# Sliding-window attention followed by a dense eight-expert MLP on one core: batch 1's token blocks offered in units of 256, and batch 2's casts and turns issued two half-blocks later

## The chip, the cores and the metric

One core of one Trainium2 chip runs the whole program in one launch. The metric is the device time of one execution in microseconds. Three runs of the kernel before took 1062.36, 1057.84 and 1061.02 us, so the median is 1061.02 us. The execution that the profiler recorded took 1060.31 us; its span, from the first to the last instruction, is 1058.5 us.

## The reference

The inputs q, k and v have 8 batches, 8 heads, 576 positions and 64 channels. Attention is causal with a window of 128 positions and a linear bias by head. Its output, 4608 tokens of 512 channels, is the input x of eight experts, all of which see every token; their outputs are weighted by a routing matrix P that eight row and column normalisations produce.

```python
scores = scale * np.matmul(q, k.transpose(0, 1, 3, 2))
mask = (rel >= 0) & (rel < window)
scores = np.where(mask, scores + bias[None], -1000000000.0)
attn = np.exp(scores)
...
logits = x @ w_gate
...
for e in range(E):
    h = np.maximum(x @ w1[e], 0.0)
    ye = h @ w2[e]
    out += P[:, e:e + 1] * ye
```

## The kernel before

**Stages.** Attention runs batch by batch, and experts 0 and 1 are computed between its pieces, so that TensorE (PE) has matmuls to do while ScalarE (ACT) and VectorE (DVE) work on the softmax. Their results go to memory (`ysp`). Then come the gating, the eight normalisations and, for most of the span, experts 2 to 7. The change touches the attention stage alone, and of it batches 1 and 2.

**Half-blocks.** A batch has five blocks of keys (`kb` 0 to 4; four of 128, one of 64) and two groups of four heads (`u`). One pair (kb, u) is a half-block; the loop of L627 goes through 80 of them, ten to a batch, numbered `at = 2 * kb + u`. This text writes (1,5) for half-block 5 of batch 1. In each, the next half-block's work is started and this one's is finished, in a fixed order that is written out by hand: when the next half-block has u = 0, the scores of both its head groups (PE, L363); the exponential of the next (ACT, L386); a first piece of filler (about 1 us); the mask multiplication of the next (DVE, L398); the values matmuls of this one (PE, L409) with the division by the sum (DVE, L436 and L437); if u is 0, the transposition of the previous block's output into `xT` (L447; for batches 0 to 2 and 7 by PE and a DVE copy, for the others by a DMA); the rest of the filler; and then, at the loop's end, loads, casts and turns for later batches. Every engine and every DMA queue works through its own instructions in this order; an instruction that waits holds up what stands behind it on its engine.

**Casts and turns.** q and k of a batch are loaded as float32 (`load_qk`, SP's queue, 1 MB each). `cast_qk(b, j)` turns a quarter of them to float16, k on ACT and q on DVE (L247, L245). For batches 0 to 2, `turn_pe` transposes a quarter on PE into a PSUM tile, which ACT (k, L326) or DVE (q, L324) copies to its place; for the later batches `turn_qk` does it by two DMA transposes on SP's queue, and POOL and DVE bring the result into order (`order_qk`). The last 64 positions of q and k travel in a tile of their own; for batches 0 to 2 PE turns it when the next half-block is (b,5), that is in (b,4), and ACT copies it out (L320). `load_qk(2)` is issued in (0,3), `load_qk(3)` in (1,3) and `load_qk(4)` in (2,3).

**Filler.** `Filler` holds units (expert, first block, number of 128-token blocks). A unit has eight L1 atoms (one eighth of the hidden width each: four matmuls over its tokens, then a ReLU on ACT, L109) and one L2 atom for each block (eight matmuls, then a copy on DVE, L499 or L495). `take` gives the next atom: two L1, then an L2 if there is one; a unit is begun, the first of the list that is ready, when no L1 atom is left and at most two L2 atoms are. A unit is ready when all its blocks are (`ready`, L659 to L664: in batches 0 to 2, block 4b + n counts as ready from the end of (b,2n), and all four from the end of (b,8)) and its expert is allowed (expert 1 from the end of (1,4)). `backlog` is the planned time of all that is ready (0.87 us for an L1 atom of four blocks, in proportion for fewer, and 1.74 us for an L2 atom), and `budget` spreads it evenly over the half-blocks up to (b,8) in batches 0 to 2, or up to the next batch's first.

**PSUM.** Filler, values, turns and gates share four PSUM buffers (`pmm`), so a matmul group can also wait for the evacuation of an earlier one. The scores have two buffers of their own (`psS`).

Of the kernel before, what the change touches and what calls it, by code (L numbers as in the profile page):

```python
# [14 lines left out]
def kernel(  # L15
# [25 lines left out]
    NG = Ntok // GT  # L41
# [161 lines left out]
    if True:  # L203
# [33 lines left out]
        def cast_qk(b, j):  # L237

            if j == 0:
                c16s[b] = per.tile([P, 2, RI, H, Dh], FP16, name=f"c16_{b}", tag="a8", bufs=8)  # L240
            for n in (1, 0):
                src = raw[b][n][:, 2 * j : 2 * j + 2, :].rearrange("p h (i d) -> p i h d", i=RI)
                to = c16s[b][:, n, :, 2 * j : 2 * j + 2, :]
                if n == 0:
                    nc.vector.tensor_copy(out=to, in_=src)  # L245
                else:
                    nc.scalar.copy(out=to, in_=src)  # L247
            if j == NDT - 1:
                raw.pop(b)
# [52 lines left out]
        def turn_pe(b, kq, j):  # L302

            wide = j == NDT
            ps = aps.tile([P, RI, P], FP32 if wide else FP16, name=f"psT_{b}_{kq}_{j}", tag="pmm", bufs=4)
            for i in range(RI):
                if wide:
                    src = tails[b][:, 2 * i : 2 * i + 2, :]
                else:
                    src = c16s[b][:, kq, i, 2 * j : 2 * j + 2, :]  # L310
                nc.tensor.matmul(
                    out=ps[:, i, :],
                    lhsT=src.rearrange("p h d -> p (h d)"),
                    rhs=ident32 if wide else ident,
                    is_transpose=True,
                    start=(i == 0),
                    stop=(i == RI - 1),
                )
            if wide:
                nc.scalar.copy(out=QKT[b][2], in_=ps)  # L320
                return
            to = QKT[b][kq][:, j].rearrange("p (r i) -> p r i", i=RI)
            if kq == 0:
                nc.vector.tensor_copy(out=to, in_=ps.rearrange("p i r -> p r i"))  # L324
            else:
                nc.scalar.copy(out=to, in_=ps.rearrange("p i r -> p r i"))  # L326
# [36 lines left out]
        def scores(b, kb, u):  # L363

            nk, nn = sizes(kb)
            ps = aps.tile([P, 2, 2, 2 * P], FP32, name=f"psS_{b}_{kb}_{u}", tag="psS", bufs=2)
            both = kb < NKB - 2
            for y in range(2):
                j = 2 * u + y
                for hb in range(2):  # L370
                    n = 2 * P if both else nk
                    nc.tensor.matmul(  # L372
                        out=ps[0:nk, hb, y, 0:n],
                        lhsT=cols(b, 1, j, hb, kb),
                        rhs=cols(b, 0, j, hb, kb, 1 + both),
                    )
                for hb in range(2):
                    if nn and not both:
                        nc.tensor.matmul(
                            out=ps[0:nk, hb, y, nk : nk + nn],  # L380
                            lhsT=cols(b, 1, j, hb, kb),
                            rhs=cols(b, 0, j, hb, kb + 1),
                        )
            pss[b, kb, u] = ps

        def exps(b, kb, u):  # L386
            nk, nn = sizes(kb)
            ps = pss.pop((b, kb, u))
            pt = asb.tile([P, 4, 2 * P], FP16, name=f"pt_{b}_{kb}_{u}", tag="pt", bufs=4)
            nc.scalar.activation(  # L390
                out=pt[0:nk, :, 0 : nk + nn],
                in_=ps[0:nk, :, :, 0 : nk + nn].rearrange("p a y n -> p (a y) n"),
                func=AF.Exp,
                scale=scale,
            )
            pts[b, kb, u] = pt

        def masks(b, kb, u):  # L398
            nk, nn = sizes(kb)
            pt = pts[b, kb, u]  # L400
            hs = slice(4 * u, 4 * u + 4)
            w = nk + nn
            nc.vector.tensor_tensor(  # L403
                out=pt[0:nk, :, 0:w], in0=pt[0:nk, :, 0:w], in1=mask[0:nk, hs, 0:w], op=ALU.mult
            )
# [38 lines left out]
        def by_pe(b):  # L444
            return b < XPE or b == B - 1
# [53 lines left out]
            nc.vector.tensor_copy(out=yo, in_=ps)  # L499
            stores.append((e, blk, yo))  # L500

        spans = [(0, 2), (2, 2)] + [(4 * g, 4) for g in range(1, NG)]
        order = [(0, 0), (0, 1)]
        for n in range(2, len(spans)):
            order += [(0, n), (1, n - 2)]
# [82 lines left out]
        def some(n):  # L588
            for _ in range(min(n, len(todo))):
                todo.pop(0)()  # L590
# [36 lines left out]
        for n, (b, kb, u) in enumerate(steps):  # L627
            nxt = steps[n + 1] if n + 1 < len(steps) else None
            at = 2 * kb + u
            left = ((8 if b < XPE else 10) - at) % 10 + 1  # L630
            budget = filler.backlog() / (11 if (b, at) == (XPE, 0) else left)
            if nxt:
                if nxt[0] < XPE and nxt[1:] == (RI - 2, 1):
                    turn_pe(nxt[0], 0, NDT)
                if nxt == (1, 0, 0):
                    cast_qk(1, 0)
                    cast_qk(1, 1)
                    for j in range(NDT):
                        turn_pe(1, 1, j)
                        turn_pe(1, 0, j)  # L640
                        if j < 2:
                            cast_qk(1, j + 2)
                        filler.fill(1.0)
                if n == 0:
                    scores(*nxt)
                elif nxt[2] == 0:
                    scores(*nxt)
                    scores(*nxt[:2], 1)
                exps(*nxt)
            got = filler.fill(1.0)  # L650
            if nxt:
                masks(*nxt)
            values(b, kb, u)
            if n > 0 and u == 0 and by_pe(steps[n - 1][0]):
                turn_x(*steps[n - 1][:2])
            if u == 1 and n // 2 + NKB < B * NKB:
                cast_v(n // 2 + NKB)
            filler.fill(budget - got)
            if at == 0 and b > XPE:  # L659
                filler.ready = 4 * b  # L660
            if at < 8 and b < XPE:
                filler.ready = 4 * b + at // 2
            if at == 8 and b < XPE:
                filler.ready = 4 * b + 4  # L664
            if u == 1 and not by_pe(b):
                turn_x(b, kb)
            if u == 1:
                if kb == 1 and b > 0:
                    gates(4 * b - 4, 4 * b)
                if n // 2 + NKB + 1 < B * NKB:  # L670
                    load_v(n // 2 + NKB + 1)
            if b == 0 and at == 1:
                load_weights(1)
            if b == 1 and at == 4:
                filler.allowed.add(1)
                nc.sync.dma_start(out=ysp[0, 0:RI].rearrange("m p d -> p m d"), in_=first_y[0])
            if (b, at) == (0, 3):
                load_qk(2)
            if (b, at) == (0, 7):
                homes(1)  # L680
            if (b, at) == (1, 3):
                homes(2)
            if b == 1 and 3 <= at <= 6:
                cast_qk(2, at - 3)
            if b == 1 and 4 <= at <= 7:
                turn_pe(2, 1, at - 4)
                turn_pe(2, 0, at - 4)
            if 1 <= b < B - 2 and at == 3:
                load_qk(b + 2)
            if 1 <= b < B - 2 and at >= 8:  # L690
                cast_qk(b + 2, at - 8)
            if 2 <= b < B - 1:
                if at < 2:
                    cast_qk(b + 1, at + 2)
                if at == 1:
                    turn_qk(b + 1)
                    order_qk(b + 1, 1, range(NDT))
                if at == 5:
                    turn_tail(b + 1)
                if at in (6, 7):  # L700
                    order_qk(b + 1, 0, range(2 * at - 12, 2 * at - 10))
            if b < B - 1 and at == (1 if b > 1 else 5) and b:
                load_tail(b + 1)
            if 10 * b + at >= 66:
                i = 10 * b + at - 66
                if i % 8 == 0:
                    home_last(2 + i // 8)
                (load_w2 if i % 8 < 4 else load_w1)(2 + i // 8, i % 4, 4)
            if (b, at) == (7, 0):
                todo += sums_of(2, *extras(2))  # L710
            if b == 7 and at >= 5:
                some(1)
# [270 lines left out]
        for n in range(N):  # L983
            g = units[n - 1][0]
# [62 lines left out]
```

## Time and profile before

| what | number |
|---|---|
| median of three runs | 1061.02 us |
| profiled execution | 1060.31 us |
| its span | 1058.5 us |
| DVE busy | 631.7 us (60%) |
| ACT busy | 434.5 us (41%) |
| PE waiting in the span's first 52.9 us, longest: L311 for ACT's cast (L247) | 7.0 us, 3 times |
| PE waiting from 52.9 to 112.85 us, longest: L457 for ACT's copy of the tail (L320) | 2.9 us, once |
| DMA engines' mean busy share, 50 to 60 us | 1.10 |
| the same, 80 to 90 us | 0.00 |

A row of a timeline names the start and the time of an instruction or of several alike, the engine, the source line, the operation, output and inputs, and in square brackets how long the engine had been idle before it and what ended that. PE's rows are modelled at their ends, so times between starts are used for what a group of matmuls costs. Half-blocks are found in PE's timeline by their order: scores of a new block appear in the odd half-blocks, the L473 group (gates) is in the third of batch 1 (it computes batch 0's), and so on. In the profiled execution (1,4) ends near 57.1 us, (1,9) begins with the scores of 76.74 us and (2,9) with those of 112.85 us.

### The profile page before, as it was taken

The numbers are of one execution on the slowest core, as the hardware profiler recorded it, in microseconds if no ns is written. First come the engines' busy times: TensorE is split into PE (matmuls) and PEld (weight loads), VectorE is DVE, ScalarE is ACT, GpSimd is POOL, SyncE is SP. The second block draws the span as 40 slices with busy tenths as digits, with TensorE's granted clock in tenths as the row PEclk, the third lists the DMA queues.
The fourth block names the chain that finished last, engine by engine and source line by source line (L and its number), as shares of the span: only waits on it lengthen the run. The fifth ranks groups of instructions, "written<-read, shape, count | busy, mean of one in ns | idle before, by whom it ended". The sixth has DMA issues, their size and how long they took to land.

```text
span 1058.5 us, 21148 instructions
## 1 busy us (share of the span) xinstructions
PE 1031.1 (97%) x9006; PEld 802.9 (76%) x9006; DVE 631.7 (60%) x1171; ACT 434.5 (41%) x729; POOL 77.4 (7%) x139
## 2 busy tenths in 40 slices
PE   6789999999999999999999999999999999999998
PEld 4455444444544888888888888888888888888887
DVE  4655665655687665655655655655655655555555
ACT  6556555555233333333333333333333333333332
POOL 2112032325100000000000000000000000000000
PEclk9999999999999999999999999999999999999999
DMA  9985599879992501211211210211220220220240
GB/s 226 252 221 139 114 201 218 196 154 177 182 207 70 115 23 49 71 26 46 71 39 33 70 49 23 71 39 32 71 65 7 71 68 3 71 71 1 71 90 20
DMA packets 166110, 98.55 MB, mean 93 GB/s; under 512 B 84960, under 2 KB 157440, under 8 KB 166016
## 3 DMA queue, kind: packets, MB, share of 16 engines
q1 hardware_dynamic: 151280, 79.21, 29.4%
q0 software_dynamic: 14304, 17.84, 10.2%
q8 instruction: 70, 1.15, 0.4%
q14 instruction: 24, 0.20, 0.1%
q10 hardware_dynamic: 432, 0.16, 0.1%
HBM read 87.74 MB, written 19.02 MB: 101 GB/s over the span
## 4 chain that ended last, share of the span: by engine, by line
PE 92%; DMA 4%; SPq 2%; DVE 1%; ACT 1%; issue 0%; POOL 0%; ACTq 0%
PE psh L834 36%; PE psS_m L889 31%; PE psh L102 11%; PE psy L115 10%; DMA v<-in_v_dram 2%; DMA k<-in_k_dram 2%; PE psN L426 1%; PE psS L372 1%; DMA xT<-xsb 1%; SPq L334 1%; SPq L223 0%; SPq L288 0%; PE psy L954 0%; PE psG L473 0%; ACT hT L109 0%
## 5 line engine op out<-in xcount | busy, mean ns | idle before, releaser
L841 ACT ACTIVATE hs<-psh 128x512 f16<-128x512 f32 x432 | 258.0, 597 | 453.2 <-PE psh L834 373.7
L834 PE MATMUL psh<-aux,w1l 128*128 128x256 f16 x2880 | 372.6, 273 | 0.2 <-ACT hs L841 0.2
L834 PEld LDWEIGHTS <-w1l 128*128 128x128 f16 x2880 | 281.7, 98 | 33.3 <-issue 0.5
L889 PEld LDWEIGHTS <-hs 128*128 128x128 f16 x2568 | 251.3, 98 | 29.1
L846 DVE TENSOR_TENSOR hs<-hs 128x1024 f16<-128x1024 f16 x107 | 74.1, 693 | 274.5 <-ACT hs L841 274.3
L889 PE MATMUL psS_m<-w2l,hs 128*128 128x256 f16 x1440 | 186.6, 273 | 0.0
L102 PE MATMUL psh<-xT,w1t 128*128 128x512 f16 (+1 forms) x640 | 141.1, 359 | 4.4 <-DMA xT<-xsb 1.7
L115 PE MATMUL psy<-w2t,hT 128*128 128x512 f16 x576 | 133.8, 379 | 3.4 <-DMA w2t<-in_moe_w_dram 2.8
L818 DVE TENSOR_TENSOR aux<-xT,pbc 128x1024 f16<-128x1024 f16 x108 | 131.4, 1217 | 2.5 <-DMA pbc<-ptd 2.5
L109 ACT ACTIVATE hT<-psh 128x512 f16<-128x512 f32 (+1 forms) x160 | 87.6, 556 | 100.6 <-PE psh L102 99.3
L115 PEld LDWEIGHTS <-hT 128*128 128x128 f16 x576 | 53.7, 98 | 64.6 <-issue 4.8
L102 PEld LDWEIGHTS <-w1t 128*128 128x128 f16 x640 | 57.9, 99 | 53.6 <-issue 6.4
L390 ACT ACTIVATE pt<-psS 128x1024 f16<-128x1024 f32 (+2 forms) x80 | 67.5, 852 | 45.9 <-PE psS L372 37.0
L935 DVE TENSOR_TENSOR acc<-acc,psS_m 128x256 f32<-128x256 f32 (+1 forms) x162 | 74.3, 504 | 12.4 <-PE psS_m L889 11.1
L499 DVE CAST yo<-psy 128x512 f16<-128x512 f32 x68 | 46.9, 690 | 55.5 <-PE psy L115 54.3
L403 DVE TENSOR_TENSOR pt<-pt,mask 128x1024 f16<-128x1024 f16 (+2 forms) x80 | 50.2, 627 | 41.5 <-ACT pt L390 41.4
L889 PE MATMUL psS_m<-more,hs 128*128 128x256 f16 x576 | 74.6, 273 | 0.0
L834 PE MATMUL psh<-aux,w1t 128*128 128x256 f16 x576 | 74.6, 273 | 0.0
L849 DVE TENSOR_TENSOR hs<-hs 128x1024 f16<-128x1024 f16 x107 | 73.2, 684 | 0.0
L834 PEld LDWEIGHTS <-w1t 128*128 128x128 f16 x576 | 56.4, 98 | 6.5
L535 POOL DMA_DIRECT2D w2t<-in_moe_w_dram x2 | 1.8, 878 | 705.2 <-PE psS_m L889 669.8
L426 PEld LDWEIGHTS <-pt 128*128 128x128 f16 (+2 forms) x576 | 28.6, 101 | 26.1 <-DVE pt L403 6.8
(83 smaller groups left out, 657.2 us busy)
## 6 DMA issues: line engine op xcount, KB each, us to landing
pbc<-ptd SPq DMA_DIRECT2D x108, 128.0 KB, 4.5
y<-ysp SPq DMA_DIRECT2D x36, 256.0 KB, 4.7
ysp<-yo SPq DMA_DIRECT2D x68, 128.0 KB, 3.1
v<-in_v_dram SPq DMA_DIRECT2D x32, 256.0 KB, 3.9
out_dram<-acc SPq DMA_DIRECT2D x31, 256.0 KB, 2.4
q<-in_q_dram SPq DMA_DIRECT2D x7, 1024.0 KB, 6.4
k<-in_k_dram SPq DMA_DIRECT2D x7, 1024.0 KB, 9.8
w2t<-in_moe_w_dram POOLq DMA_DIRECT2D x4, 1024.0 KB, 14.7
```

What stands on the lines that cost most here:

```text
L102: nc.tensor.matmul(out=ps[:, 0:nt], lhsT=w1ts[e][:, dt, P * ft : P * ft + P], rhs=xT[:, b0 : b0 + nb, dt, :], start=(dt == 0), stop=(dt == ...
L109: nc.scalar.activation(out=st["hT"][:, ft, 0:nt], in_=ps[:, 0:nt], func=AF.Relu)
L115: nc.tensor.matmul(out=ps, lhsT=st["hT"][:, ft, P * ms : P * ms + P], rhs=w2ts[e][:, ft, :], start=(ft == 0), stop=(ft == NFT - 1),)
L390: nc.scalar.activation(out=pt[0:nk, :, 0 : nk + nn], in_=ps[0:nk, :, :, 0 : nk + nn].rearrange("p a y n -> p (a y) n"), func=AF.Exp, scale ...
L403: nc.vector.tensor_tensor(out=pt[0:nk, :, 0:w], in0=pt[0:nk, :, 0:w], in1=mask[0:nk, hs, 0:w], op=ALU.mult)
L818: nc.vector.tensor_tensor(out=xs(n).rearrange("p (d b t) -> p d b t", d=NDT, b=2), in0=xT[:, 2 * g : 2 * g + 2].rearrange("p b d t -> p d ...
L834: nc.tensor.matmul(out=ps[:, f, :], lhsT=W1L[e][:, dt, P * ft : P * ft + P], rhs=xs(n)[:, HB * dt : HB * dt + HB], start=(dt == 0), stop=( ...
L841: nc.scalar.activation(out=h[n][:, 2 * i : 2 * i + 2, :], in_=ps, func=AF.Relu)
L846: nc.vector.tensor_tensor(out=t[:, NFT : NFT + NF2, :], in0=a[:, 0:NF2, :], in1=a[:, NF2:NFT, :], op=ALU.add)
L849: nc.vector.tensor_tensor(out=t[:, NFT + NF2 : 2 * NFT, :].rearrange("p f n -> p (f n)").rearrange("p (f t) -> p f t", t=P), in0=a[:, :, P ...
L889: nc.tensor.matmul(out=Ms[g, bank][:, half, :], lhsT=left(n, m, f), rhs=W2L[e][RIGHT[m]][:, f, :], start=(e == 2 and f == 0 and half == 0) ...
L935: nc.vector.tensor_tensor(out=a, in0=a, in1=p2, op=op)
```

## The change

Two edits. The first splits the units of blocks 4 to 7, which are batch 1's, into two of 256 tokens for each of the two experts. The order list keeps its rule (expert 1 two units behind expert 0).

```diff
-        spans = [(0, 2), (2, 2)] + [(4 * g, 4) for g in range(1, NG)]
+        spans = [(2 * g, 2) for g in range(4)] + [(4 * g, 4) for g in range(2, NG)]
```

The second moves batch 2's four casts and four turns. Before, cast j is issued at the end of (1,3+j) and turn j at the end of (1,4+j). After, casts 0 and 1 are issued at the end of (1,5); turns 0 and 1 and then cast 2 at the end of (1,6); turn 2 and cast 3 at the end of (1,7); turn 3 at the end of (1,8). The number of casts and turns is the same.

```diff
-            if b == 1 and 3 <= at <= 6:
-                cast_qk(2, at - 3)
-            if b == 1 and 4 <= at <= 7:
-                turn_pe(2, 1, at - 4)
-                turn_pe(2, 0, at - 4)
+            if b == 1 and 5 <= at <= 8:
+                for j in ((), (0, 1), (2,), (3,))[at - 5]:
+                    turn_pe(2, 1, j)
+                    turn_pe(2, 0, j)
+                for j in ((0, 1), (2,), (3,), ())[at - 5]:
+                    cast_qk(2, j)
```

## The prediction

> **What bounds the kernel now.** I read the page first, then PE's waits, then the timeline of the stretch that the edits touch, then that stretch as a window.
>
> ```profile
> PE 1031.1 (97%) x9006; PEld 802.9 (76%) x9006; DVE 631.7 (60%) x1171; ACT 434.5 (41%) x729; POOL 77.4 (7%) x139
> ...
> PE   6789999999999999999999999999999999999998
> ```
>
> PE is busy for 1031.1 of 1058.5 us. Its 27.4 us of idle time lie mostly in the first two slices (26.5 us each), where nothing is changed. An edit that moves PE's work without adding any can win only the idle time of its own stretch.
>
> ```profile
> 52.90:112.85 59.95, 56.05 (x484) 32.45 (x484) 33.87 (x81) 33.44 (x62) 12.77 (x27) 0.97 0.75 185
> 112.85:140.90 28.05, 26.45 (x222) 12.94 (x221) 17.05 (x40) 17.44 (x27) 6.76 (x9) 1.00 0.54 120
> 46.86:52.90 6.04, 3.97 (x73) 2.77 (x73) 5.62 (x15) 2.96 (x3) 0.00 (x0) 1.00 1.15 220
> ```
>
> Windows; the columns are length, busy time of PE, weight load, DVE, ACT and POOL, PE's clock, DMA share and rate. Up to 52.90 us (in half-block (1,4)) both kernels issue the same work; from (2,9), whose scores start at 112.85 us, the planner issues the same again. Between the two lie 3.9 us of idle PE, and the granted clock is 0.97.
>
> ```profile
> 52.49 0.39 PE L426 MATMUL psN<-v,pt 128*128 128x65 f16 x7 [0.38 <-DVE pt L403]
> ...
> 54.62 0.62 ACT L247 CAST c<-k 128x512 f16<-128x512 f32 x1 [2.90 <-DMA k<-in_k_dram]
> 55.14 0.58 ACT L320 CAST tT<-psT 128x512 f16<-128x512 f32 x1
> 55.62 1.03 ACT L390 ACTIVATE pt<-psS 128x1024 f16<-128x1024 f32 x1
> 55.77 0.59 PE L457 MATMUL psX<-ident,xsb 128*128 128x128 f16 x4 [2.89 <-ACT tT L320]
> ```
>
> This is the stall: ACT reached cast 0 of batch 2 at the end of (1,3), k's load landed only at 54.6 us, and the tail's copy and the next exponential stood behind it. PE needed the copy.
>
> **What is saved.** I measure from 52.90 us to 113.95 us, where (2,9)'s filler starts: 61.05 us. Moved to the end of (1,5), the cast no longer stands ahead of the copy. By then k has landed, as (1,5) holds 7 us of filler. Saved: 52.90 to 55.77, 2.87 us. The granted clock is 0.50 from 55.7 to 59.1 us; the groups from 55.77 to 59.35 took 3.58 us, and the same ones later, at full clock, take 0.22 (L457) + 0.45 (two turns) + 0.45 (scores) + 0.87 (two L1 atoms) = 1.99, so 1.59 us are saved if the clock stays up. PE's other waits of the stretch are 0.60 at 64.83, 0.43 at 83.25 and 0.49 at 113.95. Together 5.98 us, the most that can be won.
>
> The Trainium skill (TensorE: Matmul & The Clock Gate, Part 1) has the clock halved after an idle window of about 3.4 us in a free-running count. Here a gap of 2.87 us sufficed, as 52.3 to 55.7 was idle but for 0.4 us. By the page, the 1.59 us would not be in every execution of the kernel before, and the saving between 4.39 and 5.98 us.
>
> **The units.** At the end of (1,4) eight blocks are now ready (expert 0: 4, 5; expert 1: 0 to 5) where there were four (expert 1: 0 to 3). A block costs the planner 0.87 x 8/4 + 1.74 = 3.48 us, so the backlog is 27.84 us instead of 13.92, spread over four half-blocks: (1,5) to (1,8) get 6.96 us each, not 3.48. The ten from (1,9) to (2,8) then share 13.92 us, not 27.84; following `take`: 1.30, 1.30, 1.30, 2.17, 2.61, 0.87, 0.87, 1.74, 1.74 and 0. PE's matmuls hardly cost more: six L1 atoms of 256 tokens take 2.62 us (59.59 to 62.21), three of 512 take 2.59, so 32 x 0.437 - 16 x 0.863 = **+0.2 us**. ACT gets 32 ReLUs of 0.42 (four in 1.69) for 16 of 0.59 (two in 1.18): +4.0 us, beside PE, since ACT is busy for 33.4 of 59.95; without that cover up to +4.0.
>
> **New waits.**
> (a) Expert 0's unit of blocks 4 and 5 comes first, so (1,5) starts with matmuls on block 5, whose transposition is issued just before. Tail copy on ACT 52.1, exponential 52.6, mask 53.66 (1.06 after the exponential, as 55.62 to 56.68 before), division 54.3 and 54.5, DVE's copy to `xT` 54.8 to 55.25. PE has the turn and the scores of block 3 until 53.9. Wait 1.3, with 0.15 ahead of the turn: **+1.45 us**, none if PE arrives later, no more than the old 2.87.
> (b) Turn 3 of batch 2 now stands right ahead of (1,9)'s scores, which need its copies. DVE has a `yo` copy (0.6) and then the q copy (0.6) after the last L2; PE waits **0.7 us** (0 to 1.2, both copies). Before, (1,8) lay between.
> (c) The thin half-blocks. Without filler, four half-blocks took 6.04 us (46.86 to 52.90) with PE idle for 2.07, DVE busy for 93%: 0.52 idle each. With 2.4 us of filler, the eight from 112.85 to 140.90 had 1.60: 0.20 each. Ten of them with 1.39: between 2.0 and 5.2 us. Following the queues by hand I find 1.2 in (2,0), where the ReLUs stand behind a cast and an exponential on ACT, 0.9 in (2,2) to (2,5), and about 2 in (2,8), which has no filler while DVE still has (2,6) and (2,7)'s two `yo` copies and four reorderings (0.55 each). I take **4.0**, nearer the upper row since (2,4) to (2,8) are nearest to it.
> (d) Batch 4's load. SP works in order:
>
> ```profile
> 89.59 5.05 SPq L261 DMA_TRANSPOSE qk<-c  x2
> ...
> 98.39 0.63 SPq L232 DMA_DIRECT2D q<-in_q_dram  x1
> 99.07 1.13 SPq L232 DMA_DIRECT2D k<-in_k_dram  x1
> ```
>
> The transposes wait for batch 3's last cast, in (2,1); k's load stands 9.5 us behind them and lands 9.4 us later, near 108.5. ACT's cast of it, the last thing in (2,8), ran at 108.94: 19.4 us after the casts, with no wait. The fuller (1,5) to (1,8) put (2,1)'s end at about 96.5, and the thin (2,2) to (2,8) last some 15.5 us, not 19.4. So the cast at about 112 waits until 115.4, with (2,9)'s exponential and ReLUs behind it. PE has (2,9)'s filler (2.6 us) and values meanwhile. I take **+1.0** of the 3.5 (bounds 0 and 3.5).
>
> Nothing else of a moved step costs: casts (0.51 ACT, 0.33 DVE) and turns (0.45 PE a pair, 0.5 and 0.6 to copy) are as many as before, they issue no DMA, and `load_qk(3)`, now ahead of the cast's tile, finds free buffers. POOL's 4.6 us of reordering moves 7 us later and ends near 108, ahead of the scores at 112.
>
> **The sum.** 0.2 + 1.45 + 0.7 + 4.0 + 1.0 = 7.35 given back, against 5.98: **+1.4 us**. From (2,9) on PE has the same work and nearly no idle time, so the difference lasts to the end. 1060.31 + 1.4 = 1061.7; the median of the runs lies 0.7 above the profiled execution: **1062.4 us**, a change too small to measure (about 0.5%, 5.3 us, is what a measurement of this kernel can tell from none).
>
> **The rivals.**
> *The thin half-blocks stay full and the load is in time.* (c) at 2.0 and (d) at 0: 4.35 - 5.98 = -1.6, so 1059.4. For it: DVE's average load there, about 85%, leaves room. Against: a half-block with no filler at all.
> *The stall is won and hardly anything given back*: 0.2 + 1.45 - 5.98 = -4.3, 1056.7. It needs (b) to (d) at nothing; three queues speak against it.
> *Slower: ACT's wait for k moves from batch 2's cast to batch 4's.* Place: the end of (2,8). It decides once less than 18.9 us (9.5 + 9.4) lie between (2,1)'s casts and that cast. Price: 3.5 us with nothing to cover it, (c) at 5.2, and a clock window at half speed, 1.59, as the same wait cost before: 0.2 + 1.45 + 0.7 + 5.2 + 3.5 + 1.59 - 5.98 = +6.7, 1067.7. For it: SP's order, and that `load_qk(4)` has no slack now. Against: PE has 2.6 us of filler at that place, where it had none before.
> *It doesn't do what it says*: the casts still meet an unlanded load at (1,5). Then nothing is saved but (b) to (d) are paid: about +5.9 less part of the waits that were counted twice. 54.6 us against 62 speaks against it.
>
> **The numbers.** Forecast 0.48 (1059.5 to 1065), the full half-blocks 0.22, the stall won for nothing 0.08, batch 4's load 0.20, not done 0.02. Faster than 1055.7 takes the second rival and a quieter execution: 0.07. Slower than 1066.3 is the third, the fourth and little of the forecast: 0.21. The rest, 0.72, is no change. Range: from just under the second rival's time to just over the third's, 1056.5 to 1068.
>
> **What would show it.** In the profile after: ACT's L320 right behind the tail's turn with PE idle under 0.3 us there, and clock 1.00 at 56 us (saving); PE's first L102 after the scores near 53.5 waiting for DVE's L465 (a); scores of (1,9) waiting for L324 (b); PE's idle time between about 87 and 113 us (c); ACT's L247 waiting for k near 112 us (d). I am wrong if (1,9) starts far from 87 us, or if PE's idle time from 52.9 us to (2,9) differs from 6 to 7 us by more than 3.

## The result, and the profile after

The changed kernel took 1064.8 us in the median of 16 runs (1061.88 to 1067.18); the kernel before, over 16 runs, 1060.37 us (1056.66 to 1063.49). The ratio is 1.0043, with a 95% interval of 1.0031 to 1.0055: slower by 4.6 us, just inside the half per cent that counts as no change here, and clear of zero. The profiled execution took 1061.88 us, the lowest of its 16, with a span of 1060.1 us against 1058.5; it shows where the time goes but not all of it.

First the page of the changed kernel: busy times, and PE's clock in 40 slices.

```profile
PE 1035.0 (98%) x9070; PEld 810.4 (76%) x9070; DVE 632.4 (60%) x1171; ACT 436.8 (41%) x745; POOL 78.2 (7%) x139
...
PEclk9999899999999999999999999999999999999999
```

PE has 64 more matmuls and ACT 16 more instructions, as the units of 256 tokens ask for. PE is busy for 3.9 us more, although its work grew by 0.2 us; one slice of the clock has dropped, the fifth (106 to 132 us).

PE's timeline of the changed kernel, from the tail's turn on:

```profile
52.48 0.56 PE L457 MATMUL psX<-ident,xsb 128*128 128x128 f16 x4
...
55.02 1.03 PE L102 MATMUL psh<-xT,w1t 128*128 128x256 f16 x8 [1.27 <-DVE xT L465]
...
88.19 0.28 PE L372 MATMUL psS<-qN,kN 64*128 64x256 f16 x2 [0.50 <-ACT c L247]
...
92.66 0.60 PE L102 MATMUL psh<-xT,w1t 128*128 128x256 f16 x4 [0.96 <-ACT hT L109]
...
106.15 0.42 PE L426 MATMUL psN<-v,pt 128*128 128x65 f16 x8 [0.51 <-DVE xsb L437]
...
112.67 0.31 PE L426 MATMUL psN<-v,pt 64*64 64x65 f16 x4 [1.35 <-DVE pt L403]
...
115.29 1.86 PE L102 MATMUL psh<-xT,w1t 128*128 128x512 f16 x4 [0.67 <-DVE xT L465]
```

The stall of 2.89 us ahead of L457 is gone, and each wait that the prediction gave a letter stands where it was put: (a) at 55.02, (b) at 88.19, (c) at 92.66, 106.15 and 112.67. (2,9)'s filler starts at 115.29, 1.34 us after the 113.95 of the kernel before. But its first four matmuls take 1.86 us, not 1.02. The kernel before had at that place:

```profile
113.95 1.02 PE L102 MATMUL psh<-xT,w1t 128*128 128x512 f16 x4 [0.49 <-DVE xT L465]
```

The windows of the changed kernel (length, PE, weight load, DVE, ACT, POOL, clock, DMA share, rate) show why; the first two lie between the gates (L473) of batches 0 and 1, and of batches 1 and 2:

```profile
50.76:101.67 50.91, 47.60 (x454) 32.74 (x451) 26.36 (x62) 31.02 (x68) 5.14 (x16) 1.00 0.61 142
101.67:135.19 33.52, 30.42 (x254) 15.74 (x252) 19.61 (x48) 18.12 (x30) 8.88 (x15) 0.90 0.71 164
...
113.00:121.00 8.00, 7.19 (x32) 2.75 (x33) 4.15 (x12) 2.73 (x4) 1.93 (x6) 0.57 0.92 159
...
110.59:114.00 3.41, 2.04 (x28) 1.15 (x26) 3.38 (x9) 0.38 (x1) 0.28 (x1) 1.00 1.13 336
```

From 114.0 to 120.8 us PE ran at half its clock, after 3.41 us in which it had been busy for 2.04. In the kernel before, the clock is 1.00 all the way between the gates of batches 1 and 2, and PE waits for 0.91 us, not 3.10:

```profile
94.87:131.30 36.43, 35.52 (x285) 17.86 (x284) 21.55 (x51) 20.38 (x32) 8.59 (x15) 1.00 0.67 159
```

By the gates of batch 2 the changed kernel is 3.89 us later than the kernel before (135.19 against 131.30, not allowing for the 0.28 us by which it was ahead at batch 0's gates). Then 2.5 us come back, because the kernel before waited in this stretch and the changed kernel hardly did. PE's timeline of the kernel before at the start of batch 4:

```profile
150.38 0.30 PE L426 MATMUL psN<-v,pt 128*128 128x65 f16 x4 [0.25 <-DVE pt L403]
150.61 0.61 PE L372 MATMUL psS<-qN,kN 64*128 64x256 f16 x8
152.93 1.02 PE L102 MATMUL psh<-xT,w1t 128*128 128x512 f16 x4 [1.70 <-DMA xT<-xsb]
```

With 0.68 us at 137.93 that is 2.63 us of waiting, most of it for a DMA transposition of batch 3's output; in the changed kernel PE idled for 0.16 us between the gates of batches 2 and 3. These waits belong to this execution: a second profile of the kernel before, shown below, needs 29.62 us for the stretch, not 31.52, and has no wait for that DMA.

Why PE waits at 112.67 and 115.29 stands in DVE's timeline of the changed kernel:

```profile
110.61 1.22 DVE L272 COPY qN<-qk 128x512 f16<-128x512 f16 x2
111.75 0.68 DVE L499 CAST yo<-psy 128x512 f16<-128x512 f32 x1
112.35 0.27 DVE L403 TENSOR_TENSOR pt<-pt,mask 64x256 f16<-64x256 f16 x1
...
113.09 1.09 DVE L272 COPY qN<-qk 128x512 f16<-128x512 f16 x2
...
114.83 0.41 DVE L465 COPY xT<-psX 128x512 f16<-128x512 f16 x1
```

DVE goes from one to the next without a gap: two reorderings, a copy of an L2 atom and then the mask that PE's values need, again two reorderings and then the copy to `xT` that (2,9)'s filler needs. This is (2,6) to (2,8), where PE had too little to do.

SP's queue of the changed kernel, and behind it ACT's cast of batch 4:

```profile
96.79 4.62 SPq L261 DMA_TRANSPOSE qk<-c  x2
...
104.78 0.69 SPq L232 DMA_DIRECT2D q<-in_q_dram  x1
105.93 1.14 SPq L232 DMA_DIRECT2D k<-in_k_dram  x1
```

```profile
115.58 0.62 ACT L247 CAST c<-k 128x512 f16<-128x512 f32 x1 [4.12 <-DMA k<-in_k_dram]
```

The wait for k has moved from batch 2's cast to batch 4's, as the third rival said: the transposes were expected at 96.5 and the cast at 115.4. What the wait costs is another matter.

### The profile page after: what moved, and what is told of

It reads as the page before. It is cut to its first block, busy times and chain, and to the rows that moved or that the text cites. A ratio compares the mean times of both kernels' runs of the same rounds, so it can differ in the third digit from the quotient of the medians.

```text
span 1060.1 us, 21294 instructions
## 1 busy us (share of the span) xinstructions
PE 1035.0 (98%) x9070; PEld 810.4 (76%) x9070; DVE 632.4 (60%) x1171; ACT 436.8 (41%) x745; POOL 78.2 (7%) x139
## 4 chain that ended last, share of the span: by engine, by line
PE 93%; DMA 3%; DVE 2%; ACT 1%; issue 0%; POOL 0%; SPq 0%; DVEq 0%
PE psh L835 35%; PE psS_m L890 31%; PE psy L115 12%; PE psh L102 11%; PE psN L426 2%; DMA w2t<-in_moe_w_dram 2%; PE psS L372 1%; DMA pbc<-ptd 1%; DMA v<-in_v_dram 1%; DVE pt L403 0%; ACT pt L390 0%; PE psT L311 0%; DVE yo L499 0%; PE psG L473 0%; PE psy L955 0%; DMA k<-in_k_dram 0%
## 5 line engine op out<-in xcount | busy, mean ns | idle before, releaser
L102 PE MATMUL psh<-xT,w1t 128*128 128x512 f16 (+1 forms) x704 | 144.7, 347 | 4.6 <-DVE xT L465 3.0
L109 ACT ACTIVATE hT<-psh 128x512 f16<-128x512 f32 (+1 forms) x176 | 89.8, 521 | 103.9 <-PE psh L102 101.9
L102 PEld LDWEIGHTS <-w1t 128*128 128x128 f16 x704 | 65.1, 100 | 52.3 <-issue 10.1
L835 PEld LDWEIGHTS <-w1t 128*128 128x128 f16 x576 | 56.4, 98 | 6.5
```

The lines of the kernel that those rows point to most:

```text
L102: nc.tensor.matmul(out=ps[:, 0:nt], lhsT=w1ts[e][:, dt, P * ft : P * ft + P], rhs=xT[:, b0 : b0 + nb, dt, :], start=(dt == 0), stop=(dt == ...
L109: nc.scalar.activation(out=st["hT"][:, ft, 0:nt], in_=ps[:, 0:nt], func=AF.Relu)
L835: nc.tensor.matmul(out=ps[:, f, :], lhsT=W1L[e][:, dt, P * ft : P * ft + P], rhs=xs(n)[:, HB * dt : HB * dt + HB], start=(dt == 0), stop=( ...
```

## The experiments

**Each edit alone.** The first kernel has the change of `spans` only, the second the moved casts and turns only.

```diff
...
+        spans = [(2 * g, 2) for g in range(4)] + [(4 * g, 4) for g in range(2, NG)]
```

> The kernel before with the first edit alone (units of 256 tokens for blocks 4 to 7); batch 2's casts and turns stay where they were. Theory A (the thin half-blocks from (1,9) to (2,8) cost time, partly through the granted clock, and the moved casts win some of it back): the stall of 2.9 us at 52.9 us stays, the wait for block 5's transposition hides in it, and PE's idle time around 112 us and a half-speed stretch near it appear as in the changed kernel, so 4 to 9 us over the kernel before, ratio 1.004 to 1.0085, and not below the changed kernel's. Theory B (the loss comes from the moved casts and turns, which stand ahead of (1,9)'s scores): the units alone cost 0.2 us on PE, ratio 0.999 to 1.001.

Measured: 1066.06 us, ratio 1.0053 (1.0036 to 1.0071). The units alone lose all that the whole change loses, and theory B falls. In this profile the clock halves at 117.7 us.

```diff
...
+            if b == 1 and 5 <= at <= 8:
+                for j in ((), (0, 1), (2,), (3,))[at - 5]:
+                    turn_pe(2, 1, j)
+                    turn_pe(2, 0, j)
+                for j in ((0, 1), (2,), (3,), ())[at - 5]:
+                    cast_qk(2, j)
```

> The kernel before with the second edit alone (batch 2's casts and turns two half-blocks later); the units stay at 512 tokens. Theory A: the 2.87 us stall and the half-speed stretch behind it go, the filler's rates in batch 2 stay at 2.6 us a half-block, and only the wait of (1,9)'s scores for turn 3's copies (about 0.5 us) and perhaps 1.3 us for a later v tile (cast on POOL at 60.1 us) come back: 2 to 5 us under the kernel before, ratio 0.995 to 0.998. Theory B: 1 to 5 us over it, ratio 1.001 to 1.005.

Measured: 1058.92 us, ratio 0.9989 (0.9975 to 1.0003). The sign fits theory A, the size does not: 1.2 us, and not told apart from nothing, where 2 to 5 were expected. In its profile two waits come back, both named in the expectation: 0.5 us ahead of (1,9)'s scores and 0.93 us, at 60.68, for a v tile that POOL casts. And the stall is not the same in every execution. ACT's timeline of the units alone, where the cast still stands in its old place:

```profile
53.45 1.02 ACT L390 ACTIVATE pt<-psS 128x1024 f16<-128x1024 f32 x1 [1.59 <-PE psS L372]
54.37 0.61 ACT L247 CAST c<-k 128x512 f16<-128x512 f32 x1
55.79 0.58 ACT L320 CAST tT<-psT 128x512 f16<-128x512 f32 x1 [0.81 <-PE psT L311]
```

There is no wait for k at all, and the wait for block 5, which was expected to hide behind it, is there (1.26 us, at 58.97). In that execution PE had run at half speed for 4.8 us by batch 0's gates, which came at 54.2 us instead of 51.05, and k, which landed at about 54.1 us, was in time.

**Batch 4's load early.** The changed kernel with `load_qk(4)` at the end of (2,0), ahead of the transposes:

```diff
-            if 1 <= b < B - 2 and at == 3:
+            if 1 <= b < B - 2 and at == (0 if b == 2 else 3):
                 load_qk(b + 2)
```

> The changed kernel with batch 4's loads of q and k issued at the end of (2,0), ahead of batch 3's transposes in SP's queue, instead of (2,3). ACT's wait of 4.1 us for k at 111.5 us goes in every theory. Theory D (that wait is where the time is lost, as the third rival had it): 3 us or more come back, ratio to the kernel before 1.002 or less. Theory A (PE loses its time to the thin half-blocks and to the granted clock there, and ACT's wait lies beside PE at half speed): at most 1.5 us come back, ratio 1.003 to 1.0045.

Measured: 1065.06 us, ratio 1.0048 (1.0032 to 1.0064), just above theory A's range. ACT's wait is gone; its cast of k in (2,8) now follows the work before it:

```profile
116.67 0.61 ACT L247 CAST c<-k 128x512 f16<-128x512 f32 x1
```

Nothing came back that the runs can tell; by the two intervals together, up to some 1.6 us could have, but not 3. The wait of 4.1 us lay beside PE, which had (2,9)'s filler and ran it at half speed. Theory D falls, and with it the price of the third rival.

**The old rate.** The changed kernel with batch 1's budget held at what the kernel before gave:

```diff
+            if b == 1:
+                budget = min(budget, 3.48)
```

> The changed kernel with the planner's budget in batch 1 held at 3.48 us for a half-block, the rate of the kernel before, so that (1,5) to (1,8) get 13.9 us of filler and the ten half-blocks after them 27.8; units, casts and turns as in the changed kernel. Theory A (thin half-blocks): PE's idle time around 112 us and the half-speed stretch there vanish; the wait for block 5's transposition (1.3 us) and perhaps one for a v tile near 60 us stay: 1 to 4 us under the kernel before, ratio 0.996 to 0.999. Rival (small units or the late turns cost the time, whatever the rate): 1.003 or more, as in the changed kernel.

Measured: 1061.05 us, ratio 1.0010 (0.9997 to 1.0022). Most of the loss goes with the rate: the step from 1.0043 to 1.0010 is 3.5 us. Theory A holds on this point, though the kernel is not 1 to 4 us faster than the one before. The wait for block 5 stays (1.26 us, at 55.68). Its window between the gates of batches 1 and 2 has the clock at full speed throughout, and PE waits for 0.91 us of it, not 3.10:

```profile
94.57:131.03 36.46, 35.55 (x310) 20.20 (x308) 22.23 (x53) 21.80 (x40) 8.62 (x15) 1.00 0.65 160
```

**Expert 1 first.** The kernel with the old rate, and its first unit in (1,5) one whose blocks were long ready:

```diff
-            order += [(0, n), (1, n - 2)]
+            order += [(0, n), (1, n - 2)] if n > 2 else [(1, 0), (0, 2)]
```

> The kernel with the capped rate, and in addition expert 1's unit of blocks 0 and 1 ahead of expert 0's unit of blocks 4 and 5 in the list, so that (1,5) starts on blocks that were ready long before. Theory W (the wait for block 5's transposition, 1.3 us, is what the capped kernel has over the casts alone): that wait goes, ratio 0.9985 to 1.0 to the kernel before. Rival U (small units cost by their ReLUs and PSUM buffers wherever they run): 1.0005 to 1.0015, as with the capped rate.

Measured: 1059.27 us, ratio 0.9991 (0.9979 to 1.0004). The wait for block 5 is gone, as PE's timeline of (1,5) shows:

```profile
57.22 0.23 PE L372 MATMUL psS<-qN,kN 64*128 64x128 f16 x2
57.28 0.21 PE L379 MATMUL psS<-tT,kN 64*128 64x64 f16 x2
57.42 1.05 PE L102 MATMUL psh<-xT,w1t 128*128 128x256 f16 x8
```

The ratio is 0.0019, or 2.0 us, lower. That agrees with theory W; the two intervals overlap by a little, so the size is uncertain. The small units themselves cost nothing that could be seen.

**The half speed.** Six matmuls with unused results in (2,8):

```diff
+            if (b, at) == (2, 8):
+                psD = aps.tile([P, GT], FP32, name="psD", tag="pmm", bufs=4)
+                for i in range(6):
+                    nc.tensor.matmul(out=psD, lhsT=ident, rhs=xT[:, 0], start=(i == 0), stop=(i == 5))
             values(b, kb, u)
```

> The changed kernel with six more matmuls of 512 columns (1.3 us at full clock) in (2,8), where PE waited for DVE for 1.35 us; their result is not used. Theory C (part of the loss is the half-speed stretch that follows the thin half-blocks: 3.4 us of it in the units alone, 6.8 us in the changed kernel, none in the casts alone or with the capped rate): the busier (2,7) to (2,9) keep the clock up, no half speed between 105 and 125 us, and 1 to 3 us come back, ratio 1.0015 to 1.0035. Rival (idle time alone is the loss, the clock follows something else): the added matmuls fill idle time that was there anyway, half speed stays, ratio 1.004 to 1.0055.

Measured: 1063.51 us, ratio 1.0033 (1.0018 to 1.0048). The ratio lies in theory C's range, but the half speed stayed: 3.41 us of it, from 119.4 us, behind 3.41 us in which PE had been busy for 2.41. Inconclusive; the interval overlaps that of the changed kernel. So four such matmuls in each of (2,4) to (2,8):

```diff
+            if b == 2 and 4 <= at <= 8:
...
+                for i in range(4):
+                    nc.tensor.matmul(out=psD, lhsT=ident, rhs=xT[:, 0], start=(i == 0), stop=(i == 3))
```

> The changed kernel with four more matmuls of 512 columns, their result unused, in each of (2,4) to (2,8): 20 of them, 4.3 us at full clock, of which the idle time there (about 3 us) can hold some. Theory C (the half-speed stretch of 3.4 to 6.8 us that every profile with thin half-blocks shows follows from their low activity, and is a part of the loss): no half speed between 95 and 125 us, the added work is paid back by 1.7 to 3.4 us, ratio 1.002 to 1.004. Rival (half speed there has another cause): the stretch stays and 1.3 us or more of the added work lies on the path, ratio 1.0045 to 1.008.

Measured: 1066.7 us, ratio 1.0065 (1.0051 to 1.0079). The windows between the gates of batches 1 and 2, first of this kernel, then of a second profile of the changed kernel:

```profile
106.95:139.18 32.23, 31.21 (x273) 16.91 (x272) 19.49 (x48) 18.35 (x30) 9.06 (x15) 1.00 0.73 170
```

```profile
106.60:138.87 32.27, 29.13 (x253) 15.41 (x252) 19.44 (x48) 18.01 (x30) 8.93 (x15) 0.95 0.72 169
```

With 4.3 us of matmuls more, the stretch is not longer: idle time falls from 3.1 to 1.0 us and the half speed is gone. So in these two profiles the half speed goes with PE's low activity. What it costs in this stretch is, as an estimate, some 2 us by this sum (4.3 - 2.1) and at most 1.7 by its length (half of 3.41). The end of the kernel is another matter: the ratio fell in the rival's range, not in theory C's. This profile then waits 1.5 us for a DMA transposition at batch 4's start, which the changed kernel's did not, and has 10.24 us of half speed from 51.9 us, ahead of the added matmuls. How much of the 4.6 us at the end is due to half speed is therefore not settled.

**The same kernels again, one profile each.**

> The changed kernel once more, for a second profile. Theory A: PE idles for 3 us or more between about 100 and 120 us and the clock is halved for at least 3.4 us near its end, whatever the first 50 us did.

The changed kernel took 1066.69 us, with 3.14 us of idle PE between the gates of batches 1 and 2 (2.65 between 100 and 120 us) and 3.41 us of half speed from 119.9 us, much as expected.

> The kernel before once more, for a second profile. If k's landing is fixed by the DMA engines while the work ahead of it shifts by some us with the clock, ACT's wait for k near 53 us is shorter than 2.9 us wherever the gates of batch 0 come later than at 51.05 us, and with it the half-speed stretch behind it. If the stall is the same in every execution, it is 2.9 us again and the 5.98 us of the prediction could be won each time.

The kernel before took 1059.18 us. ACT's wait for k was 2.08 us, with batch 0's gates at 51.93:

```profile
54.29 0.62 ACT L247 CAST c<-k 128x512 f16<-128x512 f32 x1 [2.08 <-DMA k<-in_k_dram]
```

Gates at 51.05, 51.93 and 54.20 us thus go with waits of 2.90, 2.08 and none. But the landing of k is not fixed. In the DMA views of the twelve profiles of this case (time of issue and time to landing) it lies between 53.3 and 56.8 us, and from 0.1 us before batch 0's gates, in the units alone, to 3.5 us after them, in the first profile of the kernel before; the mean is 2.2 us after, and in nine of the twelve it is 1.5 us or more. By this measure a cast in its old place would mostly have had to wait, and the execution that the prediction read is the one with the longest way to k's landing. The clock was halved from 57.0 to 60.4 us all the same, and also from 50.1 to 53.5 us, before the wait had begun, so half speed here needs no stall. From batch 0's gates to batch 3's this execution needed 109.31 us, where the first profile of the same kernel needed 111.77: two executions of one kernel differ here by more than most terms of the sum.

**The casts alone, turn 3 earlier.** Against the kernel with the casts alone:

```diff
-                for j in ((), (0, 1), (2,), (3,))[at - 5]:
+                for j in ((), (0, 1), (2, 3), ())[at - 5]:
...
-                for j in ((0, 1), (2,), (3,), ())[at - 5]:
+                for j in ((0, 1), (2, 3), (), ())[at - 5]:
```

> The second edit alone, with casts 2 and 3 together at the end of (1,6) and turns 2 and 3 together at the end of (1,7), so that turn 3's copies are done well before (1,9)'s scores: the wait of 0.5 us there goes. If the casts alone win about 1 us by their stall and give 0.5 back at turn 3, this is the fastest kernel of all by a little, ratio to the kernel before 0.9975 to 0.9995. If the stall is as often absent as present, 0.9985 to 1.0005.

Measured: 1059.56 us, ratio 1.0001 (0.9992 to 1.0011). The wait ahead of (1,9)'s scores is gone, but the kernel is not the fastest, and the ratio lies in the range for a stall that is absent as often as not. Of two ways to move the casts one gave 0.9989 and the other 1.0001, with intervals that overlap: on whole runs, moving the casts is worth little. No kernel tried beats the one before by more than its interval.

## Why the prediction was right, and where its terms were not

No change was forecast, at 1062.4 us in a range of 1056.5 to 1068; 1064.8 us was measured. The direction of the sum was right, and so was nearly every place in it: (1,9) at 87.19 us (87 expected), the transposes at 96.79 (96.5), batch 4's cast at 115.58 (115.4), (2,9)'s filler 1.34 us late (1.4). PE's idle time from the tail's turn to (2,9)'s scores was 4.8 us, where 6 to 7 were expected. As the change of time it was too small, +1.4 us against about +4.6, and terms were wrong in both directions.

- **What is saved, 5.98 us, was mis-sized.** It came from one execution, the one in which k landed latest after batch 0's gates. The moved casts alone measured 1.2 us in one version and -0.1 in the other. Some of the saving is in the profiles: from batch 0's gates to batch 1's the two versions needed 41.05 and 41.10 us, the two profiles of the kernel before 43.82 and 43.26. Why so little of these 2 to 3 us is left in the medians of the runs, no run shows. The sentence on the Trainium skill (TensorE: Matmul & The Clock Gate, Part 1), by which the 1.59 us of half speed would not be in every execution, is not borne out so far: both profiles of the kernel before have 3.41 us of half speed behind the stall, from 55.7 and from 57.0 us.
- **(a), 1.45 us:** 1.27 in the profile, 2.0 (uncertain) by the two kernels with the old rate. The clock may add to it: in four of the seven profiles that have this wait, the eight matmuls behind it took 1.73 to 1.87 us, at half speed, and in the others 1.03 to 1.05. Whether the wait is the cause was not tested.
- **(b), 0.7:** 0.50. The row names ACT's cast, which the scores do not need; DVE's copy of q (87.46 us, 0.68) ended at the same time.
- **(c), 4.0:** the idle time came where it was expected, 0.96 in (2,0), 0.51 in (2,5), 1.35 in (2,8), 2.8 us in all. What was missing is the half speed behind the same thin half-blocks: 3.4 us in four of the five profiles in which they are not filled, or in (2,8) alone, and 6.8 in the fifth; none there in the six profiles with the old rate. The sum knew the clock only as a saving, and as a part of the third rival's price. So the step that the difference at (2,9) lasts to the end failed: in the first profiles of the two kernels it was 1.34 us there and 3.89 at batch 2's gates. Together, idle time and clock, the rate is worth 3.5 us by the runs.
- **(d), 1.0:** the wait came, 4.1 us long, and its cost is not to be seen: the early load gave nothing back, to within some 1.6 us. That excludes the rival's 3.5 us, not the 1.0.
- **The +0.2 for the units, with ACT's 4 us beside PE,** was right as far as the runs tell: with old rate and order the small units measured 0.9991.

By the runs, the parts are: casts -1, order of units +2.0, rate +3.5, some 4.5 us in all, each uncertain by more than 1 us. The last two are steps in one chain of kernels and the first is what is left of it, so that they add up is no check; that the moved casts alone measured -1.2 is one. The forecast's two large errors, a saving that the runs hardly show and losses that are somewhat smaller than summed, partly cancelled; that 1062.4 us came so near is in part luck.

Of the rivals, the thin half-blocks that stay full is refuted by the profile and the stall won for nothing by the time. The third was right about the move of ACT's wait and wrong about its price. The fourth is refuted too: in the changed kernel batch 2's first cast of k ran at 62.70 us without a wait.

## What to carry to other kernels

A stall on a DMA is the difference of two times, the landing and the end of the work ahead of it, and here both moved by over 3 us from execution to execution; so look at several executions before counting it as saved. Filler that is handed out earlier is taken from later half-blocks: price those at their new, thin rate, with the clock that PE was granted in such a stretch. And a wait that grows on an engine beside PE, like the 4.1 us here, may cost nothing that can be seen where PE has filler at that place; find what PE does then before giving it a price.

## What the runs showed of the hardware

The clock was halved without a long gap. In the profiled execution of the changed kernel PE's longest wait near 114 us was 1.35 us; the 3.41 us ahead of the drop held 2.04 us of PE's busy time, with 20 of the 28 matmuls values of 65 columns or transposes, and in the second profile 1.69 us. The Trainium skill (TensorE: Matmul & The Clock Gate, Part 1) describes the drop as following an idle window of about 3.4 us, and also tells of a kernel that idled often and briefly and lost its clock again and again; here, partly busy windows of that length sufficed. The steps fit its window: but for the one in which each program ends, the half-speed stretches last 3.41, 6.83 or 10.24 us, one, two or three of them.

Busy time alone does not decide it. In the kernel before, the 3.41 us from 151.26 us, a whole number of such steps after the half-speed stretch that ends at 59.1, held 1.74 us of busy time, and the clock stayed at 1.00. What else counts, no run here shows.

Executions differ early on, and not by the clock alone. Batch 0's gates came between 50.8 and 54.2 us in the twelve profiles, from the same instructions up to there. The five latest of them had 4.7 to 5.4 us of half speed before that point; the four with none came at 50.8 to 51.9 us. But the profile with the early load came at 53.45 us with 0.9 us of it. The landing of batch 1's k moves as well: ACT waited for it in all twelve, and its cast began between 34.65 and 37.10 us, in that profile at 36.93.
